# A convolution and MLP kernel: the spectrum table without its zeros, all shift filters on the tensor engine, statistics from an early copy, and a new sequence

## The chip, the cores and the metric

The kernel runs on one core of a Trainium2 chip. The core has five engines with queues of their own: TensorE (PE; its weight loads are listed as PEld), VectorE (DVE), ScalarE (ACT), GpSimd (POOL) and SyncE (SP), which here only starts transfers. Sixteen DMA engines move data between device memory (HBM) and the on-chip memory SBUF, which has 128 partitions. Matmuls write to a second memory, PSUM, of eight banks; a result has to be copied ("evacuated") from there by ScalarE or VectorE. The metric is device time in microseconds (us).

## The reference

Two layers are computed on x of 2048 positions and 512 channels, in bfloat16. A layer adds to x first a gated long convolution and then an MLP:

```
x = A_q
for two layers:
    q = layernorm(x)
    k_shift[t] = sum over j<4 of A_k[t-j] * A_shift_k[:, j]     # causal, 4 taps a channel
    kv = k_shift * A_v
    y  = causal convolution over time of kv with A_ssm_k (2048 taps a channel, by FFT) + kv * A_ssm_D
    x  = x + q * y
    x  = x + gelu(layernorm(layernorm(x)) @ B_w1 + B_b1) @ B_w2 + B_b2
```

k, v and the filters are the same in both layers, so y is the same too, and the kernel computes it once.

## The kernel before

**Layout.** Position t = 16 p + a lies in partition p; the sixteen values of a are "slices" of 128 positions by 512 channels. Everything in SBUF lies in one tensor `ar`, whose regions (`R_...`) are given out by `place` and used again as data die; small statistics lie in `sm`, all of PSUM is `ps`.

**Convolution stage.** It is a Fourier transform in two matmul stages, over p and over a. The filter comes in with time on the free axis: "ht" transposes it on TensorE (L528) and VectorE copies it out, the term `A_ssm_D` being added to the first tap (L450). "h1" is stage one of the filter: 16 matmuls per tile that use the array as two halves of 64 columns (L545), 16 tiles. "h2" is stage two: 128 matmuls with a weight matrix each from the table `tab_s2` (region `R_S2`, 128 x 16384 values, 4 MB), eight per tile (L558). Each weight matrix is block-diagonal over four channels, so three quarters of the table are zeros. A copy of the spectrum with real and imaginary partitions exchanged (`R_HS`) is made by 16 transfers. "fir0" to "fir3" are the shift filters of four blocks of 128 channels with the product by v: blocks 0 and 1 on TensorE (`shift_pe`: transposes of k L589, copy to `R_KT`, matmuls with diagonal matrices of the taps L606, product with v from PSUM L613), blocks 2 and 3 on VectorE (`shift_tt`: four multiplications, three additions and the product with v, each of 128x2048, through L450). "x1" and "x2" are the two transform stages of kv (L545, L651), in two parts of 64 channel groups; each x2 tile is copied out and multiplied by both copies of the filter's spectrum (L450). "i1" (L674) and "i2" (L731) go back, and y lies in `R_YT`. Evacuations of all of these go through one helper (L453) to either ScalarE or VectorE; 1024 columns of f32 each in most cases.

**MLP stage.** Layer 0 runs in blocks of 1, 1, 2, 2, ... slices, layer 1 in blocks of 4. For a block: "q" takes mean and variance (L754, L756), POOL makes the reciprocal deviation (L760, L762), VectorE normalizes (L768); "y" multiplies by y and adds to x (L450); "z" takes statistics again and normalizes; the result is transposed, for the first two slices by TensorE (L814), later by a transposing DMA (L807); "m1" is the first matrix (four matmuls per tile L827, gelu on ScalarE L832), "m2" the second (L860), whose result VectorE adds to x (L864). The last slice is cut in three (L849, L853).

**Order.** Nothing is scheduled on the chip. `Prog.op` records each operation with what it reads and writes; `arrange` puts the operations on their engines in the order of the list `ORDER`, gives operations named in `SECOND` to the second engine they allow, and PSUM tiles to the banks in `BANKS`; `sync` sets a wait wherever another engine or a transfer must come first. An engine, SP included, takes its queue strictly in turn, so an operation that waits holds up all behind it.

**Start.** POOL clears a block of `R_W`, eight warm-up matmuls read it (L499); the tap rows are spread over partitions by two matmuls (L511) for VectorE's blocks, and POOL multiplies the identity by each tap for TensorE's (L520). SP loads the filter, k, v and the table in 40 transfers, which for the most part wait for nothing:

```
LOADS = ("k", "v") + tuple(range(16))
def tload(t, row, off, dst_off, n, eng=SP):
...
tload(t_s2, 128 * 128, step * 1024, R_S2 + step * 1024, 1024)
```

## Time and profile before

| | |
|---|---|
| time, median of 3 runs | 241.32 us (241.05 to 241.69) |
| profiled execution: span, first to last instruction | 238.8 us |
| its own time beside the span | not given by the page; the median is 2.5 us above the span |
| PE busy | 226.2 us, 95% |
| DVE busy | 171.6 us, 72% |
| ACT busy | 138.3 us, 58% |
| POOL busy | 41.3 us, 17% |
| evacuations L453 on ACT, on DVE (1024 columns f32) | 75 and 11 |
| granted TensorE clock | 1.000 |

Busy time counts an engine from the start to the modelled end of its instructions, and matmuls overlap each other, so that 95% does not mean a TensorE at its peak. The timeline lists instructions merged in order of time: start, length, engine, line, operation, output and input, number, and in brackets the idle time before and what ended it. The chain that ended last is the path followed back from the last instruction.

### The profile page before, as it was taken

Reading aid. Unit: us, or ns where it says so; the run is one execution under the profiler, and the core shown is the slowest. Engines: PE = TensorE matmul, PEld = TensorE weight load, DVE = VectorE, ACT = ScalarE, POOL = GpSimd, SP = SyncE. Lnnn points to the kernel's source line nnn. Section 1 sums busy time; section 2 is a strip of 40 time slices with the busy share of each in tenths; the row PEclk is TensorE's granted clock in tenths of the full one; section 3 lists DMA queues with packets and bytes.
Section 4 is the critical chain, followed back from the end, with each engine's and each line's share of the span. In section 5 each row is a group of like instructions: output and inputs, shape, how many; then the busy total and the mean of one; then the engine's idle time right before and its main releaser. Section 6 shows DMA issues by size and latency. Waiting matters only on the chain.

```text
span 238.8 us, 5555 instructions
## 1 busy us (share of the span) xinstructions
PE 226.2 (95%) x2312; PEld 151.6 (63%) x2332; DVE 171.6 (72%) x359; ACT 138.3 (58%) x225; POOL 41.3 (17%) x77
## 2 busy tenths in 40 slices
PE   7987989886999999999999999999999999999995
PEld 3875778875899886766766667644444444444543
DVE  0979999999999999999887999693793312030035
ACT  2598799999999995642754444342782042454100
POOL 2179000000013444041230310400220200000000
PEclk9999999999999999999999999999999999999999
DMA  6999949999960003111122022240013021310024
GB/s 241 364 342 383 383 148 253 249 272 309 379 227 0 3 0 68 26 23 31 37 47 44 0 48 44 45 88 3 0 22 66 3 44 31 101 44 3 0 71 148
DMA packets 37035, 27.40 MB, mean 115 GB/s; under 512 B 19506, under 2 KB 29969, under 8 KB 37010
## 3 DMA queue, kind: packets, MB, share of 16 engines
q1 hardware_dynamic: 36446, 26.91, 37.8%
q8 instruction: 18, 0.29, 0.5%
q10 hardware_dynamic: 564, 0.14, 0.4%
q14 instruction: 7, 0.06, 0.1%
HBM read 16.82 MB, written 2.10 MB: 79 GB/s over the span
## 4 chain that ended last, share of the span: by engine, by line
PE 77%; ACT 9%; DMA 4%; DVE 4%; SPq 3%; issue 3%; ACTq 0%
PE ps L860 31%; PE ps L827 30%; ACT ar L453 9%; PE ps L674 5%; PE ps L731 3%; SPq L439 3%; PE ps L545 3%; DMA ar<-in_A_ssm_k_dram 2%; DVE ar L453 2%; DMA ar<-ar 2%; PE ps L528 1%; PE ps L606 1%; PE ps L849 1%; DVE sm L754 1%; PE ps L589 1%
## 5 line engine op out<-in xcount | busy, mean ns | idle before, releaser
L832 ACT ACTIVATE ar<-ps,sm 128x256 bf16<-128x256 f32 (+4 forms) x143 | 64.7, 525 | 72.5 <-PE ps L827 68.1
L827 PE MATMUL ps<-ar 128*128 128x256 bf16 (+4 forms) x568 | 84.2, 297 | 0.2
L860 PE MATMUL ps<-ar 128*128 128x512 bf16 (+1 forms) x329 | 79.0, 379 | 0.6
L453 ACT ACTIVATE ar<-ps 128x1024 bf16<-128x1024 f32 (+1 forms) x81 | 72.5, 1057 | 9.0 <-PE ps L511 4.5
L827 PEld LDWEIGHTS ps<-ar 128*128 128x128 bf16 (+1 forms) x572 | 52.9, 100 | 29.8 <-ACT ar L832 0.5
L450 DVE TENSOR_TENSOR ar<-ar 128x512 bf16<-128x512 bf16 (+3 forms) x106 | 63.6, 634 | 2.0 <-DMA ar<-in_A_k_dram 1.3
L860 PEld LDWEIGHTS ps<-ar 128*128 128x128 bf16 (+1 forms) x341 | 33.1, 98 | 34.3 <-ACT ar L832 0.3
L864 DVE TENSOR_TENSOR ar<-ar,ps 128x512 bf16<-128x512 bf16 x31 | 20.6, 680 | 47.3 <-PE ps L860 47.3
L754 DVE BATCH_NORM_STATS2 sm<-ar 128x6 f32<-128x512 bf16 (+1 forms) x68 | 42.8, 647 | 0.1
L768 DVE TENSOR_SCALAR ar<-ar,sm 128x512 bf16<-128x512 bf16 x64 | 25.0, 407 | 7.8 <-POOL sm L762 5.2
L760 POOL TENSOR_SCALAR sm<-sm 128x2 f32<-128x2 f32 (+2 forms) x26 | 6.0, 232 | 93.9 <-DVE sm L756 93.3
L762 POOL TENSOR_TENSOR sm<-sm 128x2 f32<-128x2 f32 (+2 forms) x26 | 21.6, 832 | 2.2
L545 PE MATMUL ps<-ar 128*64 128x128 bf16 x512 | 17.1, 221 | 1.4 <-issue 0.8
L545 PEld LDWEIGHTS ps<-ar 128*64 128x64 bf16 x512 | 14.9, 110 | 3.2 <-issue 1.0
L674 PE MATMUL ps<-ar 128*128 128x128 bf16 x256 | 15.0, 220 | 0.6 <-ACT ar L453 0.6
L674 PEld LDWEIGHTS ps<-ar 128*128 128x128 bf16 x256 | 14.7, 114 | 0.8 <-ACT ar L453 0.8
L453 DVE CAST ar<-ps 128x1024 bf16<-128x1024 f32 x11 | 13.0, 1212 | 0.3 <-PE ps L558 0.3
L651 PE MATMUL ps<-ar 128*128 128x64 bf16 x256 | 9.8, 194 | 3.2 <-ACT ar L453 2.7
L453 DVE COPY ar<-ps 128x2048 bf16<-128x2048 bf16 (+1 forms) x8 | 8.2, 1024 | 6.4 <-PE ps L528 6.3
L651 PEld LDWEIGHTS ps<-ar 128*128 128x128 bf16 x256 | 8.2, 98 | 4.7 <-ACT ar L453 3.9
L756 DVE BATCH_NORM_AGGREGATE sm<-sm 128x2 f32<-128x6 f32 (+1 forms) x64 | 9.9, 171 | 0.3
L558 PE MATMUL ps<-ar 128*128 128x128 bf16 x128 | 8.6, 220 | 0.8 <-ACT ar L453 0.8
(34 smaller groups left out, 78.1 us busy)
## 6 DMA issues: line engine op xcount, KB each, us to landing
ar<-tab_s SPq DMA_DIRECT2D x16, 256.0 KB, 9.6
ar<-ar SPq DMA_DIRECT2D x16, 256.0 KB, 4.2
ar<-in_A_ssm_k_dram SPq DMA_DIRECT2D x4, 512.0 KB, 5.3
ar<-in_A_k_dram SPq DMA_DIRECT2D x8, 256.0 KB, 7.6
ar<-in_A_v_dram SPq DMA_DIRECT2D x8, 256.0 KB, 9.6
ar<-in_A_q_dram SPq DMA_DIRECT2D x4, 512.0 KB, 7.9
out_dram<-ar SPq DMA_DIRECT2D x7, 256.0 KB, 2.1
ar<-in_B_w_dram SPq DMA_DIRECT2D x1, 1376.0 KB, 12.6
```

Source lines behind the costliest of these rows:

```text
L450: return P.op(eng, lambda e: e.tensor_tensor(o, a, b, op), reads=[a, b] + list(more), writes=[o])
L453: f = {ACT: lambda e: e.activation(dst, src(), AF.Copy), DVE: lambda e: e.tensor_copy(dst, src())}
L545: r = e.matmul(Q(tl, 64 * ri, 64, i * 128, [1, 128]), w, m, start=True, stop=True)
L651: r = e.matmul(Q(tl, 0, 128, i * pitch, [1, n]), w, m, start=True, stop=True)
L674: r = e.matmul(Q(tl, 0, 128, i * 128, [1, 128]), w, m, start=q == 0, stop=q == 1)
L754: P.op(DVE, lambda e, sj=sj, x=x: e.bn_stats(sj, x), reads=[x], writes=[sj])
L762: P.op(POOL, lambda e: e.tensor_tensor(r, v, hf, ALU.pow), reads=[v, hf], writes=[r])
L768: P.op(DVE, lambda e: e.tensor_scalar(o, x, m, r, ALU.subtract, ALU.mult), reads=[x, m, r], writes=[o])
L827: r = e.matmul(Q(tl, 0, rows, 0, [1, w]), a, m, start=dk == 0, stop=dk == 3)
L832: P.op(ACT, lambda e, dst=dst, tl=tl, rows=rows, bias=bias, w=w: e.activation(dst, Q(tl, 0, rows, 0, [1, w]), AF.Gelu_apprx_tanh, bias=bia ...
L860: r = e.matmul(Q(tl, 0, 128, 0, [1, 512]), ins[fc][0], ins[fc][1], start=fc == 0, stop=fc == 10)
L864: P.op(DVE, lambda e, x=x, tl=tl: e.tensor_tensor(x, x, Q(tl, 0, 128, 0, [1, 512]), ALU.add), reads=[x], writes=[x], tile=tl)
```

## The change

1. **The table without zeros.** `tab_s2` holds only the nonzero quarter (128 x 4096 values, 1 MB). `R_S2` is cleared by 16 memsets on POOL (11) and VectorE (5), and eight transfers of 32 partitions each put 16 runs of 256 bytes per partition in place. The weights of one frequency then stand in every fourth column (`[4, 128]`), for h2 and x2 alike, and the order of the transformed rows, and of the table `U`, changes with it.
2. **All four shift filters on TensorE.** `shift_tt` and its helpers go. A block's matmuls work on 64 channels at a time, partitions 0 to 63 and 64 to 127 separately (22 per tile in place of 14), with diagonal matrices of 64 columns that POOL makes in one operation per block. The product with v is two operations per tile instead of one.
3. **Statistics of slices 0 to 3** in layer 0 come from a second copy of those slices of q, loaded at the start (`R_QE`), with one POOL step for all four. `R_QE` lies inside the region of `R_HS`, and the statistics are recorded after the transfers and the products that write `R_HS`; so they wait for these products and read what lies there by then, not q.
4. The output of x1's first part goes to k's region (`R_K`) instead of `R_4`.
5. `ORDER`, `SECOND` and `BANKS` are new throughout. On SP the first table transfer now stands 16th, behind a memset on POOL.

```diff
-    S2 = S2.transpose(0, 1, 2, 3, 5, 6, 4).reshape(128, 128 * 128)
+    S2 = S2.reshape(128, 32, 4, 32).transpose(0, 1, 3, 2).reshape(128, 4096)
...
-PE_CH, PO_CH = (0, 1), ()
-LOADS = ("k", "v") + tuple(range(16))
+LOADS = ("k", "v") + tuple(range(8))
...
-    R_KT = (R_7, R_7 + 2080)
+    R_KT = (R_7, R_7 + 2080, R_6, R_6 + 2080)
...
-    R_GX, R_Z = R_4, R_4
+    R_Z = R_4
+    GX = {d0: R_K if not d0 else R_4 + 128 * d0 for d0, n in PARTS}
...
+    R_D, R_TC, R_QE = R_2, R_2 + 512, R_2 + 1024
...
-            tload(t_s2, 128 * 128, step * 1024, R_S2 + step * 1024, 1024)
-
+            d, g = step % 4, 16 * (step // 4)
+            dst = bass.AP(ar, d * AR + R_S2 + 512 * g + 128 * d, [[4 * AR, 32], [512, 16], [1, 128]])
+            src = bass.AP(t_s2, d * 4096 + 128 * g, [[4 * 4096, 32], [128, 16], [1, 128]])
+            P.op(SP, lambda e: e.dma_start(dst.bitcast(U16), src), writes=[dst], dma=True)
+
+    for i in range(16):
+        z = A(0, 128, R_S2 + 1024 * i, [1, 1024])
+        P.op((DVE, POOL), lambda e, z=z: e.memset(z.bitcast(mybir.dt.uint32), 0), writes=[z])
+    dma(A(0, 128, R_QE, [1, 2048]), dr(A_q, 0, [16 * 512, 128], [1, 2048]))
...
-    for i in range(4 * NPE):
-        o, t = A(0, 128, R_DG + i * 128, [1, 128]), M(0, 128, M_TAP + i, [1, 1])
-        P.op(POOL, lambda e, o=o, t=t: e.tensor_scalar(o, IDN, t, None, ALU.mult), reads=[IDN, t], writes=[o])
+    for c in range(4):
+        o = A(0, 128, R_DG + 256 * c, [64, 4], [1, 64])
+        tt(o, A(0, 128, R_FO, [0, 4], [1, 64]), A(0, 128, R_TC + 4 * c, [1, 4], [0, 64]), ALU.mult, POOL)
...
-        ins = [(i, A(0, 128, R_S2 + k * 128, [1, 128]), A(0, 128, G + k * n, [1, n])) for i, k in enumerate(ks)]
+        ins = [(i, A(0, 128, R_S2 + k // 4 * 512 + k % 4, [4, 128]), A(0, 128, G + k * n, [1, n])) for i, k in enumerate(ks)]
...
-        for a8 in range(2):
+        for a0 in (0, 8):
             tl = Tile(2)
             ins = []
-            for g in (2 * a8, 2 * a8 + 1):
-                for b in (0, 1, 2, 3, -1, -2, -3):
...
+            for a in (0, 4, 1, 2, 3, 5, 6, 7, -1, -2, -3):
+                j0, j1 = max(0, -a), min(3, 7 - a)
+                k = R_KT[c] + (a0 + a) % 16 * 130 + (2 if a0 + a >= 0 else 1)
+                for r in range(2):
+                    ins.append((a, 512 * r + 64 * (a + j0), 64 * (j1 - j0 + 1), A(64 * r, 64, k, [1, 128]),
+                                A(64 * r, 64, R_DG + 256 * c + 64 * j0, [1, 64 * (j1 - j0 + 1)])))
...
+            def g(e, hs=hs, tl=tl):
+                for r, o, v in hs:
+                    x = e.tensor_tensor(o, Q(tl, 0, 128, 512 * r, [4, 16], [64, 8], [1, 4]), v, ALU.mult)
+                return x
+            P.op(DVE, g, reads=[h[2] for h in hs], writes=[h[1] for h in hs], tile=tl)
-
-    def shift_tt(i):
...
+    P.tag = "qe"
+    for s in range(4):
+        o, si, x = M(0, 128, M_QE + 24 + 2 * s, [1, 2]), M(0, 128, M_QE + 6 * s, [1, 6]), A(0, 128, R_QE + 512 * s, [1, 512])
+        P.op(DVE, lambda e, si=si, x=x: e.bn_stats(si, x), reads=[x], writes=[si])
+        P.op(DVE, lambda e, si=si, o=o: e.bn_aggr(o, si), reads=[si], writes=[o])
...
+    early = [(M(0, 128, M_QE + 24 + 2 * s, [1, 1]), M(0, 128, M_QE + 32 + s, [1, 1])) for s in range(4)]
...
-            mr = stats(sl, False)
+            mr = early[sl[0]:sl[-1] + 1] if not L and sl[-1] < 4 else stats(sl, False)
```

More of the change, by code (lines that the diff above doesn't have):

```diff
@@ L579, in bass_interleave_layers__ssm_conv_h3__mixer_channel_mlp__prompt_kernel, with shift @@
     P.tag = ""
-    def shift_pe(i):
-        c = PE_CH[i]
+    def shift(c):
         tl = Tile(2)
-        src = [A(0, 128, R_K + 1536 + 512 * a + 128 * c, [1, 128]) for a in range(16)]
+        src = [A(0, 128, R_K + 512 * a + 128 * c, [1, 128]) for a in range(16)]
         def f(e, src=src, tl=tl):
@@ L612, in g @@
-            def g(e, o=o, v=v, tl=tl):
-                return e.tensor_tensor(o, Q(tl, 0, 128, 0, [4, 32], [128, 8], [1, 4]), v, ALU.mult)
-            P.op(DVE, g, reads=[v], writes=[o], tile=tl)
-    def shift_tt(i):
-        c = DV_CH[i]
-        eng = POOL if c in PO_CH else DVE
-        acc, tmp = [A(0, 128, o, [128, 16], [1, 128]) for o in (R_TMP + 2048 * i, R_KV + 2048 * c)]
-        def tap(j, o):
-            tt(o, A(0, 128, R_K + (3 - j) * 512 + 128 * c, [512, 16], [1, 128]),
-               A(0, 128, R_SJ + 512 * i + 128 * j, [0, 16], [1, 128]), ALU.mult, eng,
-               more=halo if j else ())
-        tap(0, acc)
-        for j in range(1, 4):
-            tap(j, tmp)
-            tt(acc, acc, tmp, ALU.add, eng)
-        tt(A(0, 128, R_KV + 2048 * c, [64, 32], [4, 16], [1, 4]),
-           A(0, 128, R_TMP + 2048 * i, [4, 32], [128, 16], [1, 4]),
-           A(0, 128, R_V + 128 * c, [4, 32], [512, 16], [1, 4]), ALU.mult, eng)
+            hs = []
```

105 lines of the change are left out of this document (38 added, 67 removed), and 100 rows, old and new, of tables (BANKS, ORDER).

## The prediction

> **What bounds the kernel now.** I read first the table of busy time by stretch, then the chain that ended last, then the timeline engine by engine. From 83.08 us, when the first MLP matmul starts, to the last at 236.42 us TensorE has work in 152.45 of 153.34 us:
>
> ```profile
> 83.08:236.42 153.34, 152.45 (x936) 88.40 (x950) 97.25 (x263) 66.20 (x145) 23.29 (x42) 1.00 0.17 38
> ```
>
> (Columns: length, then PE, PEld, DVE, ACT, POOL, granted clock, DMA share, GB/s.) Busy alone proves little, since matmuls overlap, but the chain gives the pace:
>
> ```profile
> 87.19 2.23 PE ps L827 x40
> ...
> 139.00 1.75 PE ps L827 x16
> ...
> 183.58 4.76 PE ps L860 x22
> ...
> 236.41 0.29 DVE ar L853
> ```
>
> That is 56, 109 and 216 ns for 128, 256 and 512 columns. Counting the MLP so (88 x 0.056 + 308 x 0.109 + 176 x 0.216 for L827, 341 x 0.216 for L860, 3.0 for the split last slice and the transposes) gives 153 us: the MLP is solid. The change leaves its instructions alone. So the time can only move with the start of the MLP, now 83.1 us; after it come 153.3 us and a tail of 2.4.
>
> What sets that start is the convolution stage before it:
>
> ```profile
> 16.21 6.52 ACT L453 ACTIVATE ar<-ps 128x1024 bf16<-128x1024 f32 x7 [0.22 <-PE ps L545]
> 25.32 52.64 ACT L453 ACTIVATE ar<-ps 128x1024 bf16<-128x1024 f32 x58 [2.58 <-PE ps L558]
> 78.17 6.58 ACT L453 ACTIVATE ar<-ps 128x512 bf16<-128x512 f32 x8 [0.21 <-PE ps L731]
> ...
> 49.37 14.84 DVE L450 TENSOR_TENSOR ar<-ar 128x2048 bf16<-128x2048 bf16 x13
> ```
>
> ScalarE evacuates PSUM without a gap from 25.32 to 84.75 us, 0.907 us for each 1024-column tile; VectorE has no gap over 0.5 us either from 16.4 us on (1.14 us per 2048-element operation). TensorE is close behind: I count 52 us of matmuls in those 58 us. Three nearly full engines means that taking work off one of them pays only as far as the others follow.
>
> **The change, part by part.** VectorE loses the 16 operations of `shift_tt`, 16 x 1.142 = 18.3 us. It gets back: shift products of 16 half tiles at 0.60 (the 128x512 operation with PSUM, L864, has a mean of 0.68, 0.08 of it overlap) for four whole ones at 1.14, +5.0; 18 evacuations where 11 were, +8.0; one more transposed-k copy and one fewer transposed-h copy, 0; five memsets. So most of the gain is passed on to ScalarE, which goes from 79 evacuations to 74, one of them a 2048-column bf16 copy (no ScalarE row; between 0.907, one tile, and twice that; I take 1.6, nearest to twice). The memsets: POOL's 512-element memset takes 0.53 us; with twice the bytes 0.53 to 1.06, I take 0.53 as the count of elements is the same. Four of VectorE's lie before its first data, the fifth costs 0.6.
>
> TensorE gets two more channel blocks of transposes (2 x 1.07) and eight shift tiles of 22 matmuls, 4096 columns, where it had four at 1.69. Bounds for a tile: if the two 64-row halves run together, 2048 columns or 1.0 us; if one after the other, 1.75. These rows decide for the first:
>
> ```profile
> 27.62 1.69 PE L606 MATMUL ps<-ar 128*128 128x384 bf16 x13 [0.15 <-issue]
> ...
> 38.44 0.61 PE L558 MATMUL ps<-ar 128*128 128x128 bf16 x8
> 38.98 0.64 PE L545 MATMUL ps<-ar 128*64 128x128 bf16 x16
> 39.55 0.62 PE L558 MATMUL ps<-ar 128*128 128x128 bf16 x8
> 40.16 5.32 PE L545 MATMUL ps<-ar 128*64 128x128 bf16 x160
> ```
>
> L545 uses the array as two 64-column halves, and its 16 matmuls take 0.53 us, not 16 x 0.056 = 0.89. I take 1.0. The same rows price a switch of shape: start to start 0.54 and 0.57 around one L545 tile against 0.53 in a row of ten, so at most 0.04 a switch, 0.6 for the 16 that come with the row tiles. [...]
>
> The second-stage weights become strided (every fourth column). L674 already loads such weights: 114 ns each against 98, at 58 ns a matmul, so with 128 columns it costs nothing. With 64 columns (L651, 34 ns) it lies between nothing and 58 - 34 = 24 ns, 0.4 us a tile; the 16 ns difference is nearer to nothing, and ScalarE at 0.907 a tile paces that part. I charge 0.2 us in all.
>
> Transfers: 3 MB of zeros go, 0.5 MB (q for the early statistics) come. Loading now fills the DMA engines until 31 us, yet the table is late for no one except by fractions, so I give this nothing; the cover is the first stage on TensorE. The early statistics buy nothing either: the q copy lies where the swapped spectrum is written later, and in VectorE's queue they stand behind the last product, with the same 0.7 us a slice as before. One pair of POOL steps serves three blocks instead of three pairs; the two saved (0.19 + 0.6 to 0.7 us each) lie beside VectorE's work and give nothing.
>
> Now the waits, in the queues' written order. POOL clears four blocks before the warm-up operand, so the eight warm-up matmuls start at about 3.65 instead of 1.56 us, and the three first transposes end at 10.4 instead of 9.0. POOL's tap product then waits for the shift taps (9.0 us now; two places earlier, about 8.5), and three more blocks, the h corrections and two more tap products (1.2 us each, twice the 0.67 of L520 less its start) stand behind it; the first table load on SP waits for such a block, until about 15.7 us. Behind it in SP's queue are five loads of v. With 0.45 to 0.65 us an issue and 2 to 3 us to land, the last of v arrives at 23.5 us. TensorE needs from 10.4 on 16 x 0.55 + 1.17 + 1.07 + 2 x 1.0 = 13.0 us for stage one, the last transposes and the first two shift tiles, so both arrive together and ScalarE's second-stage evacuations start at 24.2 instead of 25.32.
>
> From there ScalarE has 58 x 0.907 + 1.6 + 4 x 0.54 = 56.4 us (before: 66 pieces, 59.4). Laying the queues side by side, each matmul tile behind the evacuation that frees its banks, I find it idle twice by 1.0 us (at 28, where the matmuls of one second-stage tile stand behind two x tiles that wait for VectorE, and at 41, behind the transposes of the third block) and 0.6 in crumbs: end 24.2 + 56.4 + 2.6 = 83.2, 1.5 before the present 84.75. VectorE's last product comes at 67.3 instead of 68.1. The first MLP matmul follows at 83.1 - 1.5 + 0.2 = 81.8, the end at 81.8 + 153.3 + 2.4 = 237.5, 1.3 under the span of 238.8. The page gives no time beside the span; against the median of 241.32 (2.5 more than the span, which I carry over) this is **240.0 us**.
>
> **The rivals.** Dense: the hand-offs I walked are rougher than the chip's, and ScalarE runs without a gap as it does now. Then 24.2 + 56.4 = 80.6, 4.1 earlier, or 237.2 us. For it: its 59 us without a gap today. Against: VectorE and TensorE have about 55 us of work each in the same stretch, in fixed order.
>
> Slower, the row tiles: the halves run one after the other, +0.75 a tile. Two tiles lie before 24.2 where TensorE is the limit, so the stage starts at 25.7; TensorE's work from there to the MLP (second stage 7.2, x 8.8, shift 3.2 + 6 x 1.0, products 8.8, inverse 14.9 and 7.0) rises from 56 to 60.5 us, and the MLP starts at 86.1 at the earliest, 244.3 us. It decides from about 1.25 us a tile. For it: no row here shows a 64-row tile. Against: L545.
>
> Slower, the POOL gate: the tap products stretch, and v comes late. These rows show how:
>
> ```profile
> 13.86 2.70 POOL L520 TENSOR_SCALAR ar<-ar,sm 128x128 bf16<-128x128 bf16 x4
> ...
> 16.81 7.07 POOL L520 TENSOR_SCALAR ar<-ar,sm 128x128 bf16<-128x128 bf16 x4
> ```
>
> The same operation took 0.67 us, then 1.77 once VectorE ran `shift_tt` beside it from 16.42 us. For 256 elements I took 1.2; at 3.5 the table load's wait ends 4 to 5 us later and v with it, which makes about 243.5 us. Against: VectorE now has no such operation before its first product near 42 us. [...]
>
> No change: the zeros were hidden and two engines merely trade work, 241.3.
>
> **How the numbers follow.** A difference under 0.3% (0.7 us) can't be told from none. Forecast, 238.3 to 240.5: 0.42. Dense, 236.8 to 238.3: 0.16. Within 0.7 us of now: 0.13. Row tiles one after the other or draining at switches: 0.14. POOL gate: 0.08. Longer hand-offs or weight loads than charged, 242 to 243: 0.07. So faster 0.58, same 0.13, slower 0.29. The range, 236.9 to 243.7, leaves out the upper halves of the two slow mechanisms and little below. The forecast alone has 238.3 to 240.5.
>
> **What would show it.** The MLP stretch still 153 to 154 us, starting at 81.8. Warm-up at 3.7; ScalarE's long run starting at 24.2 with two gaps of about 1 us; shift tiles of 1.0 us; the tap products under 1.5 us each on POOL; the first table load issued near 16 us; VectorE's last product near 67. Tiles of 1.7, a v later than 26 us, or gaps in the MLP would make it wrong.

## The result, and the profile after

The changed kernel takes 243.48 us (median of 7 runs, 242.89 to 244.21) against 241.69 (241.05 to 244.80) for the kernel before on the same chip: a ratio of 1.0077, with a 95% interval of 1.0056 to 1.0098. It is slower by about 1.8 us, where 1.3 us of gain was forecast. The profiled execution took 243.19 us with a span (first to last instruction) of 241.4. The ledger against the forecast, in us:

| | forecast | measured | difference |
|---|---|---|---|
| first MLP matmul | 81.8 | 84.06 | +2.3 |
| MLP, first to last matmul | 153.3 | 155.04 | +1.7 |
| tail to the end of the span | 2.4 | 2.3 | -0.1 |
| time beside the span | 2.5 | 1.8 | -0.7 |
| sum | 240.0 | 243.19 | +3.2 |

So two things went wrong: the start of the MLP is 1.0 us later than before the change, not 1.3 earlier, and the MLP, which was called solid, became 1.7 us longer.

The two spans differ by 2.6 us, the medians by only 1.8. In every later execution on record the time beside the span is 1.7 to 2.2 us, in nearly all 1.8. If it was 1.8 for the profiled execution of the kernel before too, that one took 240.6 us, less than any of its seven timed ones (241.05 at least). So up to 0.8 us of the differences between the two profiles may belong to that one execution.

The busy time of the MLP stretch (from and to, length, then PE, PEld, DVE, ACT, POOL, granted clock, DMA share, GB/s; the window ends 0.1 us before the last matmul does) goes with the second:

```profile
84.06:239.00 154.94, 153.51 (x946) 88.16 (x946) 102.69 (x264) 65.76 (x144) 22.39 (x42) 1.00 0.17 39
```

TensorE's timeline of the changed kernel (start, length, operation, idle before and what ended it; `issue` means that the profile shows nothing that was waited for) now has waits in this stretch; the same view of the kernel before has no such row:

```profile
84.06 4.19 PE L798 MATMUL ps<-ar 128*128 128x128 bf16 x72
...
108.75 3.22 PE L798 MATMUL ps<-ar 128*128 128x256 bf16 x28 [0.85 <-issue]
...
156.93 4.91 PE L798 MATMUL ps<-ar 128*128 128x512 bf16 x24 [0.22 <-issue]
...
170.52 3.63 PE L798 MATMUL ps<-ar 128*128 128x512 bf16 x16 [0.26 <-DMA ar<-ar]
```

Counted from start to start against a pace of 56, 109 and 216 ns for 128, 256 and 512 columns, four waits of 1.0, 0.4, 0.4 and 0.3 us stand near 107.9, 156.7, 170.3 and 204.4: 2.1 us. The matmuls themselves run at the old pace (for 256 and 512 columns they last 273 and 379 ns in the mean, before and after). Eleven traces of the runs below leave the MLP as it is; in them it takes 154.5 to 155.9 us, with waits (those of 0.25 us and more) of 1.3 to 2.7 us in all. So the loss recurs, but the places and sizes of the waits differ from execution to execution.

ScalarE's timeline, the one that was forecast piece by piece:

```profile
24.74 4.00 ACT L449 ACTIVATE ar<-ps 128x1024 bf16<-128x1024 f32 x4 [1.69 <-PE ps L537]
29.66 5.61 ACT L449 ACTIVATE ar<-ps 128x1024 bf16<-128x1024 f32 x6 [0.91 <-PE ps L537]
35.63 6.53 ACT L449 ACTIVATE ar<-ps 128x1024 bf16<-128x1024 f32 x7 [0.36 <-PE ps L537]
42.68 8.29 ACT L449 ACTIVATE ar<-ps 128x1024 bf16<-128x1024 f32 x8 [0.52 <-PE ps L615]
51.23 23.02 ACT L449 ACTIVATE ar<-ps 128x1024 bf16<-128x1024 f32 x25 [0.26 <-PE ps L524]
74.47 10.32 ACT L449 ACTIVATE ar<-ps 128x1024 bf16<-128x1024 f32 x13 [0.22 <-PE ps L638]
```

It starts at 24.74 (forecast 24.2) and ends at 84.79 (83.2; before 84.75). The work in it is what was forecast: 58 tiles at a pace of 0.903 us start to start, the one 2048-column copy at 1.76, four short ones at 0.48, together 56.1 us. The other 3.9 us are hand-offs (forecast 2.6): 2.3 in the brackets above, the rest in waits too short for a row of their own.

Just before the MLP, the changed kernel's chain that ended last no longer runs through TensorE alone, as it did before, but through VectorE and GpSimd:

```profile
74.47 3.35 ACT ar L449 x4
...
81.91 0.35 POOL sm L731
...
82.33 0.69 POOL sm L733
...
83.05 0.41 DVE ar L739
...
83.66 0.35 DVE ar L449
...
84.06 1.96 PE ps L798 x32
```

The first matmul needs the copy of the transposed slice 1 (L449), and in VectorE's written order this stands behind the normalization of slice 0 (L739), which waits for GpSimd. ScalarE's last evacuation ended 1.67 us after the first MLP matmul began before the change, and 0.73 us after it now.

### The profile page after: what moved, and what is told of

The parts are those of the page before. It is cut to its first block, busy times and chain, and to the rows that moved or that the text cites. A ratio compares the mean times of both kernels' runs of the same rounds, so it can differ in the third digit from the quotient of the medians.

```text
span 241.4 us, 5859 instructions
## 1 busy us (share of the span) xinstructions
PE 229.9 (95%) x2482; PEld 156.4 (65%) x2482; DVE 174.8 (72%) x367; ACT 135.4 (56%) x218; POOL 37.0 (15%) x79
## 4 chain that ended last, share of the span: by engine, by line
PE 52%; DVE 21%; POOL 6%; ACT 6%; SPq 5%; DMA 5%; issue 3%; POOLq 0%
PE ps L798 19%; PE ps L831 15%; DVE sm L725 6%; ACT ar L449 6%; DVE ar L446 5%; DVE ar L739 4%; PE ps L638 4%; SPq L778 3%; DMA ar<-ar 3%; PE ps L537 3%; POOL sm L733 3%; PE ps L584 2%; DVE ar L835 2%; PE ps L524 2%; DMA ar<-in_A_v_dram 2%
## 5 line engine op out<-in xcount | busy, mean ns | idle before, releaser
L798 PE MATMUL ps<-ar 128*128 128x256 bf16 (+4 forms) x572 | 83.1, 297 | 1.6 <-issue 1.1
L831 PE MATMUL ps<-ar 128*128 128x512 bf16 (+1 forms) x341 | 80.2, 379 | 0.0
L449 ACT ACTIVATE ar<-ps 128x1024 bf16<-128x1024 f32 (+2 forms) x74 | 69.1, 1068 | 13.2 <-PE ps L507 6.9
L446 DVE TENSOR_TENSOR ar<-ar 128x512 bf16<-128x512 bf16 (+3 forms) x90 | 46.3, 531 | 0.9
L725 DVE BATCH_NORM_STATS2 sm<-ar 128x6 f32<-128x512 bf16 (+1 forms) x64 | 40.9, 651 | 0.7
L739 DVE TENSOR_SCALAR ar<-ar,sm 128x512 bf16<-128x512 bf16 x64 | 24.1, 410 | 11.6 <-POOL sm L733 9.4
L449 DVE CAST ar<-ps 128x1024 bf16<-128x1024 f32 x18 | 21.6, 1216 | 0.7 <-PE ps L524 0.4
L733 POOL TENSOR_TENSOR sm<-sm 128x2 f32<-128x2 f32 (+2 forms) x23 | 18.7, 812 | 1.9
L524 PE MATMUL ps<-ar 128*64 128x128 bf16 x512 | 16.8, 220 | 1.2 <-DVE ar L594 0.5
L524 PEld LDWEIGHTS ps<-ar 128*64 128x64 bf16 x512 | 14.8, 110 | 2.7 <-DVE ar L594 1.0
L638 PE MATMUL ps<-ar 128*128 128x128 bf16 x256 | 15.2, 220 | 0.6 <-ACT ar L449 0.4
L638 PEld LDWEIGHTS ps<-ar 128*128 128x128 bf16 x256 | 14.6, 114 | 0.9 <-ACT ar L449 0.9
L594 DVE TENSOR_TENSOR ar<-ps,ar 128x512 bf16<-128x512 f32 x16 | 10.2, 683 | 3.3 <-PE ps L584 1.8
L449 DVE COPY ar<-ps 128x2048 bf16<-128x2048 bf16 (+1 forms) x8 | 8.1, 1016 | 6.1 <-PE ps L507 5.6
```

The source lines that it names most:

```text
L446: return P.op(eng, lambda e: e.tensor_tensor(o, a, b, op), reads=[a, b] + list(more), writes=[o])
L449: f = {ACT: lambda e: e.activation(dst, src(), AF.Copy), DVE: lambda e: e.tensor_copy(dst, src())}
L524: r = e.matmul(Q(tl, 64 * ri, 64, i * 128, [1, 128]), w, m, start=True, stop=True)
L594: x = e.tensor_tensor(o, Q(tl, 0, 128, 512 * r, [4, 16], [64, 8], [1, 4]), v, ALU.mult)
L638: r = e.matmul(Q(tl, 0, 128, i * 128, [1, 128]), w, m, start=q == 0, stop=q == 1)
L725: P.op(DVE, lambda e, sj=sj, x=x: e.bn_stats(sj, x), reads=[x], writes=[sj])
```

## Experiments

Times are medians, and ratios are to the kernel before, timed beside each of the five groups of runs (e1 to e4, e5 to e8, e9 to e12, e13 to e16, e17 and e18). It had 241.38, 241.61, 241.36, 241.85 and 242.02 us in them, so ratios are compared, not times. Their 95% intervals reach 0.3 to 0.7% to each side, and where a few tenths of a microsecond matter the profiles have to serve; each is of one execution. Numbers with # are operations, as the list `ORDER` numbers them. In the diffs `...` stands for lines left out.

### The start: warm-up, gate and early copy

**e1_warm_first.** POOL clears the warm-up operand ahead of the table blocks.

```diff
 POOL: 
-#8, #10, #11, #12 (table blocks), #304, #54 (operand), ...
+#54 (operand), #8, #10, #11, #12, #304, ...
```

> The changed kernel with one move: POOL clears the warm-up operand before the four table blocks. The warm-up then starts at about 1.6 us instead of 3.80 and the first stage on TensorE about 1.2 us earlier. Theory G (the start is set by v and the table, whose transfers on SP wait for a memset on POOL): VectorE's first shift product still waits for v, landing at 23 to 24.8 us, so ScalarE's second-stage run still starts at 24.5 to 24.8 and the time stays within 0.3 us of the changed kernel's 243.5. Rival W (the late warm-up delays everything): all 1.2 us come through, 242.3. Rival M (what was lost is lost in the MLP's order): no change either, and the idle piece of TensorE near 108 us stays.

Measured: 243.43 us, ratio 1.0094 (1.0062 to 1.0127). The warm-up started at 1.31 us instead of 3.80, and the second stage (its first matmul on TensorE) at 24.67 instead of 24.09. Nothing was gained.

**e2_no_gate.** All memsets that the table transfers wait for stand ahead of the tap products, so that the first of these transfers is issued at 8.7 us, not 14.6.

```diff
 POOL:
-... #56 (taps) ... #13, #9 ... #57 ... #14, #23, #20 ... #16, #17
+... #13, #9, #14, #23, #20, #16, #17, #56 (taps) ...
 DVE: #22 ahead of #67
```

> The changed kernel with the memsets of the table moved: POOL clears its seven later blocks in the 5.5 us in which it waits for the taps, VectorE its fifth before its first data. No transfer on SP waits for POOL any more beyond about 8 us. Theory G: v is complete by 20 us and the first half of the table too; the second shift product starts at about 23.3 instead of 24.78, ScalarE's second-stage run at 23.7 instead of 24.74, and 0.8 to 1.0 us reach the end, 242.5. Rival W: the start stays with the late first stage, gain 0.2, 243.3. Rival M: start earlier by up to 1 us but TensorE waits longer in the MLP for VectorE, 243.3.

Measured: 244.6 us, ratio 1.0119 (1.0072 to 1.0166). **e3_both** joins the two edits:

> Both moves together. Theory G: now TensorE's own first stage is the limit and it begins 1.2 us earlier; ScalarE's second-stage run starts near 22.5, 2.2 us earlier than in the changed kernel, of which 1.5 to 2 reach the end, 241.5 to 242.0. Rival W: as the first move alone plus 0.2, 242.1, with no more than the sum of the two. Rival M: the MLP starts up to 2 us earlier but does not end more than 0.5 earlier, 243.0, with more idle pieces on TensorE between 85 and 175 us.

Measured: 244.86 us, ratio 1.0135 (1.009 to 1.018). The gate is not the cause; taking it away made nothing faster. In the profiles the last of v did land earlier, at 23.58 us in e2 and 23.91 in e3 instead of 24.76. TensorE's timeline of e3_both shows what stood in its place:

```profile
5.26 2.51 PE L501 MATMUL ps<-ar 128*128 128x128 bf16 x32 [0.36 <-DMA ar<-in_A_ssm_k_dram]
...
22.72 1.81 PE L578 MATMUL ps<-ar 64*128 64x256 bf16 x41 [2.24 <-issue]
```

It began 1.9 us earlier than in the changed kernel (7.16) and then stood for 2.24 us in the middle of a shift tile, where the profile shows no data that are waited for. The section on the hardware comes back to this. The second stage started at 24.46, no earlier than with the gate. The DMA engines are full there (share 1.08 from 21 to 24 us in e3_both, 0.88 in the changed kernel), so the volume of transfers may be what bounds the start whatever the order of issue; that is argued, not shown. Nor do the profiles explain the medians of e2 and e3: that of e2 is of its fastest execution (242.7 us), and that of e3 has a wait of 1.3 us near 126.4 in the MLP, where no other trace has more than 0.5.

**e4_no_copy.** No early copy of q; the four statistics read the slices where they are loaded anyway.

```diff
-    dma(A(0, 128, R_QE, [1, 2048]), dr(A_q, 0, [16 * 512, 128], [1, 2048]))
...
-        o, si, x = M(0, 128, M_QE + 24 + 2 * s, [1, 2]), M(0, 128, M_QE + 6 * s, [1, 6]), A(0, 128, R_QE + 512 * s, [1, 512])
+        o, si, x = M(0, 128, M_QE + 24 + 2 * s, [1, 2]), M(0, 128, M_QE + 6 * s, [1, 6]), A(0, 128, R_X + 512 * s, [1, 512])
```

> The changed kernel without the early copy: the transfer of 0.5 MB at the start goes, and the statistics of the first four slices read the q slices in their usual place, in the same places of VectorE's queue (so here they are statistics of q). All theories: the copy buys nothing because the statistics stand behind the last product anyway; within 0.2 us of 243.5. If the copy's transfer delays the second half of the table, 0.3 us faster.

Measured: 243.48 us, ratio 1.0095 (1.0061 to 1.0129): no difference, as expected. The early statistics buy nothing and the copy costs nothing.

**e7_dense_table.** Zeros loaded again, no memsets, and so no gate either.

```diff
...
-    P.op((DVE, POOL), lambda e, z=z: e.memset(z.bitcast(mybir.dt.uint32), 0), writes=[z])
...
+            tload(t_s2, 16384, 2048 * step, R_S2 + 2048 * step, 2048)
```

> The changed kernel with the table loaded whole, zeros included, in eight transfers of 512 KB in the same places of SP's queue; the sixteen memsets are gone, and with them the wait of the first table transfer. Theory 'transfers bound the start': 3 MB more at the 0.36 to 0.38 MB/us that this stretch moves are 8 us of transfer, of which the part ahead of the first second-stage weights and of the last v shows; TensorE's code blocks come later too; second stage from 25.5 to 28 us, time 244 to 246.5. Theory of the recorded prediction (the zeros were hidden behind the first stage): second stage from 24 to 24.7, time 243.2 to 243.8.

Measured: 244.44 us, ratio 1.0119 (1.0063 to 1.0174), about 1 us above the changed kernel. In its profiled execution, the slowest of its five, the second stage starts at 26.64 us. So leaving the 3 MB of zeros out seems to be worth something in this kernel, in the order of 1 us; the intervals overlap, so no closer figure is claimed. In this profile TensorE's clock was at half from 24.1 to 30.9 us, so 26.64 is an untypical start.

### The MLP: order or work?

**e5_mlp_before.** The MLP's operations in the relative order of the kernel before, from the first MLP matmul on.

```diff
 per engine, from #350 on:
-block operations in the changed kernel's order
+block operations in the order of the kernel before
```

> The changed kernel's start and convolution stage as they are; from the first MLP matmul on, the operations of every engine in the relative order that the kernel before gives them (what the changed kernel puts ahead of that matmul stays there; the PSUM banks of the MLP are given out anew). Theory 'sequence': the MLP lasts 1.7 us longer only because four waits of TensorE (1.0 us at 107.5, 0.4 at 156.3, 0.4 at 169.9, 0.3 at 204.0) come with the new order, so here it lasts 153.2 to 153.8 us again, from about 84.1, and the time is 241.9 (241.4 to 242.4). Rival 'late start': VectorE brings 1 us of backlog into the MLP and loses it somewhere whatever the order; then the MLP lasts 154.5 to 155 us and the time stays at 243 to 243.6.

Measured: 243.74 us, ratio 1.0093 (1.006 to 1.0126). The MLP lasts 155.05 us, from 83.98 to 239.03: the theory "sequence" has fallen. TensorE's timeline of this run has its waits in other places:

```profile
89.70 0.81 PE L828 MATMUL ps<-ar 128*128 128x512 bf16 x3 [1.30 <-ACT ar L800]
...
94.75 4.10 PE L795 MATMUL ps<-ar 128*128 128x256 bf16 x36 [0.33 <-DMA ar<-ar]
```

**e6_z4_first.** Only the block behind the wait at 107.9 is moved up.

```diff
 DVE:  ... #527,
+#531, #533, #532, #534 (statistics z4), #572, #573, #574, #626, #537, #539 (normalizations z4),
 #414 (result addition) ...
 POOL: 
-#627, #628 (q6), #575, #576 (q5), #535, #536 (z4)
+#535, #536 (z4), #627, #628 (q6), #575, #576 (q5)
```

> The changed kernel with one place of the MLP order altered: the second statistics of block z4, their POOL pair and the two normalizations that feed its transposing transfers move ahead of the statistics for q5 and q6 and of a result addition. Theory 'sequence': the wait of TensorE near 107.5 falls from 1.0 us to under 0.2, the three smaller ones stay, the MLP lasts 154.0 to 154.2 us and the time is 242.5 (242.1 to 242.9). Rival: the moved work only hands the wait to a block behind, the MLP stays at 154.8 to 155 and the time at 243.3 to 243.6.

Measured: 243.59 us, ratio 1.0105 (1.0033 to 1.0176). The wait at 107.9 is gone, and others took its place; the MLP lasts 155.24 us:

```profile
101.84 1.92 PE L792 MATMUL ps<-ar 128*128 128x256 bf16 x16 [0.27 <-DVE ar L829]
...
115.32 2.34 PE L792 MATMUL ps<-ar 128*128 128x256 bf16 x20 [0.69 <-issue]
```

Two orders, the same loss. That speaks for an amount of work, and VectorE is the engine that feeds these blocks, with little room in the kernel before. From the first MLP matmul to 110 us it was busy for 26.39 of 26.92 us there, and in the changed kernel for 24.46 of 25.94 us (DVE is the third engine):

```profile
83.08:110.00 26.92, 26.76 (x238) 19.40 (x240) 26.39 (x78) 16.38 (x47) 9.74 (x20) 1.00 0.16 31
84.06:110.00 25.94, 25.09 (x228) 18.53 (x229) 24.46 (x69) 14.92 (x43) 7.80 (x16) 1.00 0.21 32
```

The change made VectorE less full there, since in its new order it stands for 0.86 us at 100.3, waiting for GpSimd (L733). The next two runs take work from VectorE.

**e9_short_early_stats** has the first of these two edits, **e10_short_q_stats** both.

```diff
-        o, si, x = M(0, 128, M_QE + 24 + 2 * s, [1, 2]), M(0, 128, M_QE + 6 * s, [1, 6]), A(0, 128, R_QE + 512 * s, [1, 512])
+        o, si, x = M(0, 128, M_QE + 24 + 2 * s, [1, 2]), M(0, 128, M_QE + 6 * s, [1, 6]), A(0, 128, R_QE + 512 * s, [1, 8])
...
-            cuts = [(4 * d0, 4 * w) for d0, w in PARTS] if s < NSPLIT and double and not blk[0] // len(BLOCKS0) else [(0, 512)]
+            cuts = [(4 * d0, 4 * w) for d0, w in PARTS] if s < NSPLIT and double and not blk[0] // len(BLOCKS0) else [(0, 512 if double or L else 8)]
```

> The changed kernel with the four early statistics of VectorE (slices 0 to 3, near 68 to 74 us) taken over 8 instead of 512 channels (left out: the other 504). VectorE has 4 x 0.6 = 2.4 us less to do there, nothing else changes. Theory 'VectorE backlog': when the MLP starts, VectorE has 5.4 us more of its MLP work before it than in the kernel before (102.7 us busy in the MLP against 97.3), and that, not the order, makes the waits of TensorE; then the first MLP matmul comes at 83.2 to 83.7 and the waits fall from 2.1 to under 1.2 us: time 241.9 to 242.8. Rival 'latency' (the steps of POOL and the transposing transfers, not VectorE's amount of work): waits of 1.5 to 2.2 us stay, time 243.0 to 243.6.

Measured: 244.01 us, ratio 1.01 (1.0065 to 1.0134); waits of 1.8 us, as the rival said, but well within the 1.3 to 2.7 us of the traces that leave the MLP alone. VectorE's timeline of e9 shows where its 2.4 us went, into waiting for ScalarE and TensorE ahead of the MLP:

```profile
72.44 1.23 DVE L443 CAST ar<-ps 128x1024 bf16<-128x1024 f32 x1 [1.00 <-PE ps L632]
...
79.41 0.90 DVE L440 TENSOR_TENSOR ar<-ar 128x256 bf16<-128x256 bf16 x4 [1.15 <-ACT ar L443]
```

> As the run with short early statistics, and the first statistics of all other slices in layer 0 also over 8 of 512 channels: 16 x 0.6 = 9.6 us less for VectorE between 68 and 130 us. Theory 'VectorE backlog': no wait of TensorE over 0.1 us is left before 150 us, the MLP lasts 153.0 to 153.6 us, time 241.0 to 242.0. Rival 'latency': the MLP stays above 154.2 us, time above 242.6.

Measured: 242.51 us, ratio 1.0023 (0.9988 to 1.0058). No wait of TensorE over 0.1 us is left before 150 us, and the MLP is back at its old length (153.3 us before the change), as this run's stretch shows:

```profile
85.39:239.00 153.61, 152.51 (x930) 88.38 (x946) 98.74 (x264) 65.77 (x144) 22.44 (x42) 1.00 0.18 39
```

So the time of VectorE's statistics inside the MLP makes the waits: 4.3 us less of its work there (112.8 us of durations behind the first MLP matmul, against 117.1) removes them. Work taken off before the MLP does not help, since VectorE then waits for ScalarE and TensorE. Two things stay open. A shorter statistic also reaches GpSimd sooner, so amount of work and delay along this chain are not told apart; for the delay speaks that VectorE still stands for 0.86 us waiting for GpSimd, here too, where TensorE no longer waits. And in this profile the MLP starts 1.3 us late, as the last of v landed at 25.80 us instead of 24.76; e18 below has the same MLP length from an ordinary start. The "5.4 us of backlog" in these expectations was read wrongly: the durations of VectorE's operations behind the first MLP matmul add up to 117.1 us, and to 115.6 before the change, 1.5 us more. The rest of the difference between 102.69 and 97.25 is that they overlap each other less.

**e11_before_more_stats.** The kernel before, with VectorE burdened: the first statistics of slices 0 to 3 run twice.

```diff
...
+                    if more == 2:
+                        e.bn_stats(M(0, 128, 300 + 6 * s, [1, 6]), x)
                     return e.bn_stats(sj, x)
```

> The kernel before, with the first statistics of slices 0 to 3 run twice by VectorE (the second result goes to an unused place): 4 x 0.6 = 2.4 us more for VectorE between 64 and 76 us. Theory 'VectorE backlog': VectorE has no room there (0.6 us idle from 66 to 84), so the first MLP matmul comes 0.5 to 1.5 us later and waits of 0.3 to 1.5 us appear in the MLP: 242.3 to 243.8 against 241.4. Rival 'latency': the MLP has slack for it, 241.3 to 241.9.

Measured: 244.0 us, ratio 1.0099 (1.0054 to 1.0145). So 2.4 us of VectorE's work cost the kernel before 1.3 to 3.5 us: it has no room there either. In its profile TensorE was slower for a while (13 matmuls of L606 took 3.17 us from 24.69 on, against 1.69 in the kernel before; mean granted clock 0.993, see the last section), so the start of the MLP can't be read from it. The MLP behind can: it takes 153.8 us (88.22 to 242.04), 0.5 more than before, with one wait of 0.5 us near 114.9.

**e16_products_on_gpsimd.** Six multiplications by y on GpSimd instead of VectorE.

```diff
-                    tt(zc, zc, y, ALU.mult)
+                    tt(zc, zc, y, ALU.mult, POOL if not L and 4 <= s < 10 else DVE)
```

> The changed kernel with the multiplication by y of six slices (4 to 9, layer 0) on GpSimd: VectorE has 6 x 0.43 = 2.6 us less to do between 88 and 115 us, GpSimd about 6 x 1.2 = 7.2 us more. 'VectorE backlog': TensorE's waits in the MLP fall from 2.1 to under 1.2 us, time 242.4 to 243. Rival: GpSimd's reciprocal deviations stand behind these multiplications in its queue and come 1 to 3 us later, waits stay or grow, 243.4 to 246.

Measured: 246.68 us, ratio 1.0211 (1.0177 to 1.0245). This came out as the rival said. The groups of waits between 84 and 125 us show VectorE behind GpSimd, and TensorE behind the transposing transfers that follow:

```profile
DVE ar L440 <- POOL ar L440: 5.3, 5, 1.9
PEld ps L792 <- DMA ar<-ar: 3.5, 2, 1.8
PE ps L792 <- DMA ar<-ar: 2.8, 2, 1.5
```

(Columns: us in total, times, longest.) A multiplication of 512 elements took 1.24 us on GpSimd, three times VectorE's 0.42, and it lies on the path. So this run does not decide between amount of work and delay.

### The front: which engine sets the start of the MLP?

Four runs take work off one engine or all between the first second-stage matmul and the first MLP matmul, and one moves work. That stretch takes 59.97 us in the changed kernel (24.09 to 84.06) and 58.41 in the kernel before. Counted from VectorE's second shift product, which waits for the last of v (24.78 in the changed kernel), it scatters less: 59.15 to 59.39 us in the changed kernel, e1, e2, e4, e5, e6 and e16, and 59.6 to 59.8 in e3, e9 and e10. By that count e8 below has 58.57, e12 and e13 59.21, e14 57.81 and e15 60.72.

**e8_less_shift** (TensorE, -4.9 us):

```diff
-                for a, o, n, w, m in ins:
+                for a, o, n, w, m in ins[:4 if c else 22]:
...
```

> The changed kernel with 4 of 22 matmuls in the six shift tiles of channels 128 to 511 (left out: most taps of k_shift there). That takes 18 matmuls, about 0.8 us, from each, 4.9 us of TensorE's work between 24 and 84 us, and nothing from any other engine. Theory 'TensorE bounds the front now': it has work in 57.4 of the 60 us there; without these 4.9 us ScalarE, with 57.8 us of evacuations from 24.7 on, is next, so the first MLP matmul comes at 82.1 to 82.6 and the time is 241.4 to 242.1. Rival, as recorded: ScalarE with its hand-offs sets the pace; then the first MLP matmul moves by less than 0.5 us and the time is 243.0 to 243.5.

Measured: 242.5 us, ratio 1.0044 (1.0005 to 1.0082); the stretch takes 59.23 us (24.48 to 83.71), the first MLP matmul is 0.35 us earlier. TensorE alone is not what bounds the front.

**e12_short_evacuations** (ScalarE, -4.5 us):

```diff
+        nc4 = 4 if k8 in (8, 9, 10, 11, 13, 15) else 32
-        evac(BOTH, A(0, 128, R_H + 32 * k8, [4, 8], [512, 32], [1, 4]),
+        evac(BOTH, A(0, 128, R_H + 32 * k8, [4, 8], [512, nc4], [1, 4]),
...
```

> The changed kernel with six of the filter's second-stage evacuations on ScalarE (between about 29 and 42 us) cut from 1024 to 128 columns (left out: seven eighths of the spectrum at these frequencies). ScalarE has about 6 x 0.75 = 4.5 us less to do. Theory of the recorded prediction (ScalarE's evacuations and their hand-offs set the start of the MLP): the first MLP matmul comes 2 to 4 us earlier, at 80 to 82, time 240 to 241.7. Theory 'VectorE backlog': VectorE is as full (4.9 us idle from 20 to 84, back to back from 55.5 to 68.2), so the start moves by less than 1 us, time 242.6 to 243.4.

Measured: 243.45 us, ratio 1.0101 (1.0061 to 1.0142); the stretch takes 59.93 us. What ScalarE saved it spent waiting: between 28 and 43 us it waits 3.4 us for TensorE's second-stage tiles, against 1.3 in the changed kernel, and 1.3 us for other tiles, against 0.5.

**e13_short_products** (VectorE, -4.4 us):

```diff
+            nh = 1 if not d0 else 2
-            x = A(0, 128, xo, [0, 2], [4 * nk, n // 4], [1, 4 * nk])
+            x = A(0, 128, xo, [0, nh], [4 * nk, n // 4], [1, 4 * nk])
...
```

> The changed kernel with the eight spectrum products of the first part (VectorE, near 43 to 54 us) over one copy of the spectrum instead of two, 1024 elements instead of 2048 (left out: the product with the swapped copy). VectorE has 8 x 0.55 = 4.4 us less to do. Theory 'VectorE bounds the front': from the first second-stage matmul to the first MLP matmul it takes 60.0 us now (24.09 to 84.06); here 56.5 to 58, time 240.5 to 242.3. Rival 'three equally full engines': 59 to 60 us, since TensorE and ScalarE are as full, time 242.5 to 243.4.

Measured: 243.06 us, ratio 1.0063 (1.0034 to 1.0091); the stretch takes 59.89 us. VectorE alone does not bound it.

**e14_all_short** joins the three edits.

> The three reliefs in one: short products (VectorE -4.4 us), short shift tiles (TensorE -4.9), short evacuations (ScalarE -4.5), with what each leaves out. 'Three equally full engines': only together do they count, the stretch from the first second-stage to the first MLP matmul falls to 55.5 to 57 us, time 239.5 to 241. 'VectorE bounds the front': no more than 0.7 us beyond the run with short products.

Measured: 242.28 us, ratio 1.0021 (0.9987 to 1.0054); the stretch takes 58.46 us (25.24 to 83.70), 1.5 less, not the 3 to 4.5 expected of three equally full engines. ScalarE's timeline of this run shows what is left:

```profile
30.77 4.12 ACT L443 ACTIVATE ar<-ps 128x1024 bf16<-128x1024 f32 x6 [0.91 <-PE ps L531]
...
42.70 31.21 ACT L443 ACTIVATE ar<-ps 128x1024 bf16<-128x1024 f32 x33 [0.94 <-PE ps L610]
74.12 10.31 ACT L443 ACTIVATE ar<-ps 128x1024 bf16<-128x1024 f32 x13 [0.21 <-PE ps L634]
```

From 42.70 on, ScalarE runs to 84.43 with one gap of 0.21: 41.7 us, against 42.1 in the changed kernel. The edit that shortens evacuations takes none from there.

**e15_two_evacuations_moved**: two second-stage evacuations from VectorE to ScalarE.

```diff
 SECOND (the operations given to VectorE):
-117, 129, 133, 153
+117, 153
```

> The changed kernel with two of the filter's second-stage evacuations moved from VectorE to ScalarE (VectorE -2.3 us, ScalarE +1.8, near 36 to 41 us). 'VectorE bounds the front': the stretch falls by 1 to 2 us, time 241.9 to 242.8. 'Three equally full engines': what VectorE gains ScalarE loses, 59.7 to 61.5 us, time 243.2 to 244.8.

Measured: 245.13 us, ratio 1.0156 (1.0112 to 1.02); the stretch takes 61.42 us (24.47 to 85.89). ScalarE's run:

```profile
35.97 16.84 ACT L443 ACTIVATE ar<-ps 128x1024 bf16<-128x1024 f32 x17 [0.31 <-PE ps L531]
...
76.31 10.31 ACT L443 ACTIVATE ar<-ps 128x1024 bf16<-128x1024 f32 x13 [0.21 <-PE ps L632]
```

ScalarE had 1.8 us more to do, and the stretch takes 1.45 us longer, although VectorE had 2.3 us less to do. Work added to ScalarE shows almost fully; work taken from it before 42 us does not, since TensorE is next there. So the engine that the forecast named does set the pace from 42 us on: ScalarE, with TensorE close beside it before. No run takes back the shift filters alone, so how much of the later start comes from that part of the change stays open.

**e17_copy_first** and **e18_copy_first_short_q**: the copy of slice 1 ahead of the normalization of slice 0, alone and with the short statistics of e10.

```diff
 DVE: ... #386, #421, #423, #416,
+#388 (copy z1),
 #347 (normalization z0), #418,
-#388 (copy z1),
 #349 (copy z0) ...
```

> The changed kernel with one operation moved: VectorE's copy of the first transposed block (slice 1, ready at 82.7 us) ahead of the normalization of slice 0, which waits until 83.05 for GpSimd. The first MLP matmul comes at 83.1 to 83.3 instead of 84.06. If that 0.8 us is its own loss, the time is 242.4 to 242.9; if VectorE's amount of work decides ('VectorE backlog'), TensorE waits 0.6 to 0.9 us more later in the MLP and the time is 243.1 to 243.6.

Measured: 243.87 us, ratio 1.0071 (1.0035 to 1.0106). The first MLP matmul comes 1.03 us ahead of ScalarE's end instead of 0.73 (0.66 to 0.74 in all traces with the old place): 0.3 us gained, not 0.8, and no change in the time that could be told.

> The same move together with the first statistics of all slices of layer 0 over 8 of 512 channels (left out: the other 504). 'VectorE backlog': with VectorE's work away the earlier start stays: first MLP matmul at 83.1 to 83.6, MLP 153.4 to 153.8 us, time 240.8 to 241.9, 0.6 to 1.2 below the run with short statistics alone (242.5). Otherwise 242.3 to 242.8.

Measured: 242.09 us, ratio 1.0001 (0.9965 to 1.0037), half a microsecond below e10 by the ratios, within their scatter. Its MLP takes 153.5 us from 83.79 on, with one wait over 0.1 us. With both losses eased, and only with statistics over 8 channels, the kernel comes level with the kernel before and not below it: the forecast's 81.8 is not reached by anything tried here. No version tried beats the kernel before.

## Why the prediction was wrong

- **"The MLP is solid; the change leaves its instructions alone; after its start come 153.3 us."** This is the step that turned the sign. The forecast put the waits of this stretch at nothing, and TensorE waited 2.1 us there. That TensorE is full was read rightly, but not how near VectorE is to being full beside it: to 110 us it was busy for 26.4 of 26.9 us already in the kernel before. With the change 1.5 us more of VectorE's work stands behind the first MLP matmul. e10 and e18, with less of that work and an MLP of 153.6 and 153.5 us, show that the time of VectorE's statistics makes the waits, e5 and e6 that neither other order tried avoids them; whether it is their amount or their delay on the way through GpSimd is not shown. The text did say that gaps in the MLP would make it wrong; none of its rivals had them.
- **"ScalarE idle twice by 1.0 us and 0.6 in crumbs: end 83.2."** The work was right (56.1 us for 56.4), the hand-offs were 3.9 us and not 2.6, and the start 0.5 later: end 84.79. Of the hand-offs 2.3 us stand in rows, for the two gaps of 1.0 us that were found by hand; what was undercounted most are the waits too short for a row, 1.6 us for 0.6.
- **"0.45 to 0.65 us an issue and 2 to 3 us to land: the last of v at 23.5."** Issue was right: the last of v was issued at 20.51. It landed at 24.76, 4.25 us later, and the other four behind the gate took 4.0 to 5.2. On the lists of both kernels transposing transfers land in 2.5 us and stores in 1.4 to 2.1; the medians of loads are 3.3 us and more. The product of the second tile waited for v until 24.78, and the first table weights until 24.09. The list of the kernel before has 9.6 us for such a load and would have been further off, on the other side; the three that were issued ahead of the gate here took 9.9 to 10.4 us.
- **"The first MLP matmul follows at 83.1 - 1.5 + 0.2."** This carried over a lead on ScalarE's end, 1.4 us against 83.2; the new order leaves 0.73. Of the missing 0.7 the place of one copy accounts for 0.3 (e17).
- **"2.5 more than the span, which I carry over."** Every later execution has 1.7 to 2.2 us beside its span, so this term was 0.7 too large; the span that it was added to may have been untypically short by as much (see the result).
- **"Transfers: I give this nothing."** Leaving out the zeros seems to be worth about 1 us in the new kernel (e7), and the second stage starts 0.6 us earlier than before (24.09 against 24.67). It brought no gain in the end.
- **Row tiles: right that both halves run together, wrong on the switches.** In TensorE's timeline shift tiles stand between second-stage pieces:

```profile
32.41 1.05 PE L584 MATMUL ps<-ar 64*128 64x256 bf16 x22
33.40 0.64 PE L537 MATMUL ps<-ar 128*128 128x128 bf16 x8
33.97 1.05 PE L584 MATMUL ps<-ar 64*128 64x256 bf16 x22
```

  That is 0.99 us from start to start for 22 matmuls, 1.0 forecast; 2048 columns at 109 ns for 256 are 0.87, so both halves run together. But the eight matmuls between the tiles take 0.57 us for 8 x 0.056 = 0.45, so each change of shape costs about 0.1 us: behind a 128-column matmul on the whole array the first on halves of it (L584, L524; L545 in the kernel before) starts 0.15 us later where nothing else is waited for, one of the same shape 0.056 us later, and on the way back from L584 to L537 it is 0.12 us. The prediction's "at most 0.04 a switch" came from setting an L558 tile (eight matmuls, 0.45 us without a switch) against a row of L545 tiles (0.53). Its 16 switches cost about 1.5 us of TensorE's time, not 0.6; with TensorE alone relieved by 4.9 us for a gain of 0.7 (e8), little of that reaches the end. A draining at switches, which has a share in the 0.14 of the chances, is shown by no run; the traces show these 0.1 us a change, and not what makes them.
- **POOL gate: rightly small.** The tap products took 0.61 us instead of 1.2, the memsets 0.52, and the first table transfer was issued at 14.63 for 15.7. With the gate gone (e2) v landed 1.2 us earlier, but nothing improved.
- **Early statistics buy nothing, strided weights cost next to nothing: right** (e4; 48 matmuls of 64 columns in 1.76 us).

## What to carry to other kernels

A stretch that one engine fills need not be solid: the MLP here grew from 153.3 to 155.04 us with its instructions unchanged, so look for the second-fullest engine in the first part of the stretch before carrying its length over. Where three engines are nearly full, price a change by the work that it adds to each of them in the stretch where that one leads; relief of one engine alone was worth 0 to 0.7 us of 4 to 5 here, and 1.8 us added to the leading one cost 1.5. A transfer's landing time is not one figure: loads of 256 KB took 4.0 to 5.2 us and 9.9 to 10.4 us within one execution here, so it enters a forecast as a range. A profile is of one execution: set its time against the timed ones before small differences are read from it.

## What the runs showed of the hardware

**TensorE stops at the same two places.** The stops marked "issue" in the first 25 us stand at two places only, counted in matmuls of the trace: ahead of the 222nd and of the 348th, 126 further on. This holds for both kernels, whatever operation stands there: in the kernel before L545 (15.60) and a transpose of k (22.08), in the changed kernel L524 (16.77) and the fourth matmul of the first shift tile (21.71). The page lists transfers in a queue of the kind "instruction", 16 KB each: 18 in the kernel before and 19 in the changed one, for 4644 and 4964 instructions of PE and PEld, so 258 and 261 to a transfer; 126 matmuls with their weight loads are 252. The first two ended at 14.11 and 20.66 us in the kernel before and at 15.52 and 20.04 in the changed one, each 1.2 to 1.7 us before TensorE went on. So it may be waiting for its own instructions there; this is read from the times and was not tried by moving either place. The stops took 0.79 and 1.31 us in the kernel before, 0.46 and 0.32 in the changed kernel and 0.40 and 2.24 in e3_both; e10 and e18 have none at the second place. The DMA engines had a share of 0.88 from 21 to 24 us in the changed kernel, and of 1.06 and 1.08 in the kernel before and e3_both, where the second stop is longer. In the run with the dense table, with a share of 1.01 to 1.06 from 14 to 24 us, the two stops are:

```profile
16.65 1.83 PE L515 MATMUL ps<-ar 128*64 128x128 bf16 x59 [1.57 <-issue]
...
23.10 2.46 PE L575 MATMUL ps<-ar 64*128 64x256 bf16 x41 [1.83 <-issue]
```

**Three profiled executions had a lower clock for a while.** The busy time of the same run, with the granted clock as the third number from the right (1.00, then 0.52 and 0.50):

```profile
22.00:24.00 2.00, 0.90 (x24) 0.90 (x25) 0.00 (x0) 0.92 (x2) 0.00 (x0) 1.00 1.01 398
24.00:26.00 2.00, 1.56 (x23) 1.27 (x17) 1.29 (x2) 0.00 (x0) 0.00 (x0) 0.52 1.05 411
...
28.00:30.00 2.00, 2.00 (x27) 1.80 (x27) 1.77 (x2) 1.32 (x2) 0.00 (x0) 0.50 1.04 206
```

The clock stayed at half for 6.8 us here (24.1 to 30.9) and for 3.4 us in e17 (25.7 to 29.1); e11, with the slow matmuls of L606 from 24.69 on, has the same mean clock as e17 (0.993, in e7 0.986). These three profiled executions were the slowest of their runs (246.31 to 246.44 us). Shortly before, TensorE had stopped for 1.83 us in e7 (until 23.10), for 1.84 us in e17 (until 24.52), and for 1.38 and 1.24 us in e11 (until 22.44 and 24.69). But in e3, with a stop of 2.24 us until 22.72, the clock was 1.00 from 9 to 30 us, and e10, with one of 1.81 us until 27.17, has a mean clock of 1.000. So the length of a stop does not tell these cases apart, and what makes the clock fall is not shown.

How much time goes with a lower clock is on record, as the mean clock of each timed execution: of the 98 of the kernel before in the five groups, 20 had 0.992 or 0.993 and a median of 243.5 us, the other 78 had 0.999 or 1.000 and 241.5. A stretch of 3.4 us at half the clock, as in e17, takes 0.7% off the mean clock of 242 us, which is the missing 0.007. These 20 are the upper part of the scatter of the kernel before (242.3 to 244.7 of 240.5 to 244.7 us).
